# Spreading a routing chain over many steps, one pipeline for the output blocks, and loads a job ahead, in a one-core attention and routed-FFN kernel

## The chip, the cores and the metric

The kernel runs on one core of one Trainium2 chip, in one launch; the host only lays arrays out. The metric is the device time in microseconds of one execution, over several runs. A profiled execution has a span (first to last instruction) beside its own time.

## The reference

Two branches over the same tokens are mixed by a gate. S = 2048 tokens, D = 640, 32 heads of 20, four segments of 512 tokens. Cut to what matters:

```python
g = sigmoid((x * gate_w).sum(-1, keepdims=True))
# A: segment-wise attention with a compressive memory
q, k, v = x @ wq, x @ wk, x @ wv           # 32 heads of 20
for s in range(4):                         # segments of 512
    a_dot = softmax(qs @ ks.T * scale + causal_mask) @ vs
    a_mem = (phi(qs) @ M) / (phi(qs) @ z + 1e-6)
    o = sigmoid(beta) * a_mem + (1 - sigmoid(beta)) * a_dot
    M, z = M + phi(ks).T @ vs, z + phi(ks).sum()
a = o @ wo
# B: one routed token goes through a SwiGLU FFN (F = 1728)
r = x @ w_r
idx = argmax(r)
y = (silu(x[idx] @ w_gate) * (x[idx] @ w_up)) @ w_down * sigmoid(r[idx])
b = x + (y added at row idx)
return g * a + (1 - g) * b
```

All of it is float32; the large products are made from rounded high parts and remainders.

## The kernel before, in words

The work is cut into eight units u, each one half of the heads (16) in one segment of 512 tokens. A unit has nine projection jobs, T0 to T4 (rows of q and k, transposed, 512 tokens wide) and V0 to V3 (values, 128 tokens each), in the order `JOBS`. A job is 15 matmuls: five blocks of the 640 inputs, and for each the three products of high and low parts. High and low parts are made by `split`: ScalarE copies the loaded tile to the rounded type (hi), and VectorE or GpSimd subtracts it (lo). T weights come by `prepare_t`, V and O weights by `load_w` and `split_w`, x by `load_x` and `split_x`. In every one of these the load stands directly in front of the split. All loaded tiles (raw), and in the output stage the tiles ot and xf, share one ring of four buffers.

`evac_t` moves a finished T job out of PSUM: hi on ScalarE, lo on VectorE, then phi in three steps. `place` stores hi and lo to DRAM scratch (stkq, stkk) and `bring_back` loads them into the layout for attention (qs, ks). `keys`, `memory_read` and `memory_write` serve the compressive memory.

Attention runs over 32 groups n of four heads (four to a unit). A group has six slots: `a_step` makes scores for the row maxima, which VectorE reduces (mx); `m_rows` writes the negative maxima into qs by four small DMAs (qs<-mr); `b_step` makes the scores again, transposed and with the maxima subtracted, ScalarE takes the exponential, GpSimd masks the diagonal; `pv_phase` multiplies with the values in two halves (slots 1 and 5). `norm` divides, and `store` puts the result in the DRAM tensor otok.

TensorE's and SP's queues are in the order in which the Python program emits instructions; the other engines' order is set by the scheduler. The program interleaves generators by hand: `fill` lets the projections run ahead of the attention by a fixed lead, `extra` fills with output work, and `side` takes one step of the FFN in each half PV phase:

```python
def pv_phase(n, half):
    pv_step(n, half)
    for f in side:
        f.run(1.0)
```

At group 15 `route` finds the top token: a maximum per partition, a column out to DRAM (rrow<-best) and back as a row, a maximum, one value out and back to all partitions, twice over. At group 16 `fetch` loads that token's row and the FFN starts: `ffn_up` for gate and up (10 steps), `ffn_act`, `ffn_down` (8 steps, a pair of weight tiles wt each, from a ring of two buffers), then the row y goes to DRAM and comes back to all partitions (yb). At group 28 `finish()` emits what is left of it.

The output stage has 16 blocks t of 128 tokens. `row_load` loads otok's rows (ot), `out_load` loads x's rows (xf) and mixes them with the FFN's row, `out_rows` transposes and splits, `out_proj` runs 30 matmuls (L649) and stores. It treats four blocks at a time; inside the four, block t+1's loads are emitted at the start of block t, after the store of block t-1. Three fours run between the attention's instructions, the last four after its end.

## Time and profile before

| | |
|---|---|
| median of 3 runs | 819.74 us (819.0 to 822.08) |
| profiled execution, its own time | 825.51 us |
| its span | 823.8 us |
| TensorE busy | 691.1 us (84%) |
| VectorE, ScalarE, GpSimd busy | 442.0, 361.6, 188.7 us |
| mean granted TensorE clock | 0.901 of full |
| DMA | 116.30 MB, mean 141 GB/s |

In the views, PE is TensorE, PEld its weight load, DVE VectorE, ACT ScalarE, POOL GpSimd, SP the queue that issues all DMAs. L351 is line 351 of the kernel; `acc<-xhi,whi` names the tile written and the tiles read. A row of a timeline is: start in us, duration in us, engine, line, operation, tiles, shapes, count, and in brackets how long the engine was idle before and what released it. Rows of the chain that ended last have start, duration and what ran. A "releaser" is inferred from semaphores.

### The profile page before, as it was taken

Reading aid. Unit: us, or ns where it says so; the run is one execution under the profiler, and the core shown is the slowest. Engines: PE = TensorE matmul, PEld = TensorE weight load, DVE = VectorE, ACT = ScalarE, POOL = GpSimd, SP = SyncE. Lnnn points to the kernel's source line nnn. Section 1 sums busy time; section 2 is a strip of 40 time slices with the busy share of each in tenths; the row PEclk is TensorE's granted clock in tenths of the full one; section 3 lists DMA queues with packets and bytes.
Section 4 is the critical chain, followed back from the end, with each engine's and each line's share of the span. In section 5 each row is a group of like instructions: output and inputs, shape, how many; then the busy total and the mean of one; then the engine's idle time right before and its main releaser. Section 6 shows DMA issues by size and latency. Waiting matters only on the chain.

```text
span 823.8 us, 13347 instructions
## 1 busy us (share of the span) xinstructions
PE 691.1 (84%) x4496; PEld 468.9 (57%) x4496; DVE 442.0 (54%) x1523; ACT 361.6 (44%) x608; POOL 188.7 (23%) x297
## 2 busy tenths in 40 slices
PE   5478989989998997885598999898989588797876
PEld 3355566556665664553355665565656376475766
DVE  6426546655665775553355666674667355442323
ACT  4234545645564665541344455454545333242211
POOL 4002311522342233121131133323422111021000
PEclk9689989999998997897698999998999879797879
DMA  5546453644475474700786477547765612233323
GB/s 157 145 106 186 118 141 97 167 110 117 125 187 146 106 184 127 207 13 14 187 246 187 136 243 219 161 147 197 208 180 149 184 42 80 89 105 104 104 100 124
DMA packets 80627, 116.30 MB, mean 141 GB/s; under 512 B 37478, under 2 KB 41072, under 8 KB 80560
## 3 DMA queue, kind: packets, MB, share of 16 engines
q1 hardware_dynamic: 80560, 115.46, 49.7%
q8 instruction: 36, 0.59, 0.3%
q14 instruction: 31, 0.25, 0.1%
HBM read 72.94 MB, written 41.96 MB: 139 GB/s over the span
## 4 chain that ended last, share of the span: by engine, by line
PE 52%; DMA 19%; DVE 9%; ACT 7%; issue 6%; SPq 4%; POOL 1%; POOLq 0%; DVEq 0%; ACTq 0%
PE acc L351 13%; PE pv L454 7%; PE acc L649 7%; PE bt L434 7%; PE acc L356 7%; PE a L403 5%; DVE junk L406 3%; DMA xf<-in_x_dram 3%; DMA raw<-in_xT_dram 3%; DMA qs<-mr 3%; DMA stkq<-lo 3%; PE nm L266 3%; DVE lo L241 2%; DMA rrow<-best 2%; ACT hi L240 1%
## 5 line engine op out<-in xcount | busy, mean ns | idle before, releaser
L406 DVE CUSTOM_DVE_ANT_0 junk<-a,mask 128x512 bf16<-128x512 f32 (+3 forms) x512 | 250.2, 489 | 147.9 <-PE a L403 137.9
L438 ACT ACTIVATE p<-bt 128x768 f32<-128x768 f32 (+1 forms) x192 | 169.3, 882 | 187.0 <-PE bt L434 183.0
L441 POOL TENSOR_SCALAR_AFFINE_SELECT p<-p 128x256 f32<-128x256 f32 (+1 forms) x192 | 94.7, 493 | 402.3 <-ACT p L438 399.4
L434 PE MATMUL bt<-qs,ks 62*128 62x256 f32 (+2 forms) x512 | 100.0, 421 | 25.4 <-DMA qs<-mr 23.3
L351 PE MATMUL acc<-xhi,whi 128*128 128x512 f32 x200 | 89.7, 449 | 24.2 <-ACT xhi L149 15.1
L403 PE MATMUL a<-ks,qs 60*128 60x256 f32 (+2 forms) x512 | 84.7, 361 | 20.8 <-DVE mx L406 16.0
L351 PE MATMUL acc<-xhi,wlo 128*128 128x512 f32 x200 | 93.6, 468 | 0.5 <-DVE wlo L150 0.4
L434 PEld LDWEIGHTS bt<-qs,ks 62*128 62x128 f32 x512 | 47.1, 198 | 82.5 <-issue 41.5
L351 PE MATMUL acc<-xlo,whi 128*128 128x512 f32 x200 | 90.9, 454 | 1.6 <-POOL xlo L150 1.5
L454 PE MATMUL pv<-p,va 128*32 128x512 f32 (+3 forms) x1024 | 85.3, 452 | 0.0
L150 POOL TENSOR_TENSOR xlo<-raw,xhi 128x512 fp32r<-128x512 f32 x38 | 47.9, 1283 | 95.8 <-DMA raw<-in_xT_dram 62.4
L403 PEld LDWEIGHTS a<-ks,qs 60*128 60x128 f32 x512 | 50.3, 202 | 33.2 <-DVE mx L406 22.5
L351 PEld LDWEIGHTS acc<-xhi,whi 128*128 128x128 f32 x200 | 41.1, 206 | 45.9 <-ACT xhi L149 17.4
L649 PE MATMUL acc<-whi,oh 128*128 128x320 f32 x160 | 57.9, 362 | 4.9 <-ACT oh L626 3.4
L649 PE MATMUL acc<-whi,ol 128*128 128x320 f32 x160 | 56.1, 351 | 0.4 <-DVE ol L627 0.2
L356 PE MATMUL acc<-wlo,xhi 128*128 128x322 f32 (+1 forms) x160 | 56.2, 351 | 0.0
L351 PEld LDWEIGHTS acc<-xlo,whi 128*128 128x128 f32 x200 | 41.1, 205 | 25.2 <-issue 15.1
L356 PE MATMUL acc<-whi,xhi 128*128 128x322 f32 (+1 forms) x160 | 54.9, 343 | 0.0
L649 PE MATMUL acc<-wlo,oh 128*128 128x320 f32 x160 | 54.7, 342 | 0.0
L356 PE MATMUL acc<-whi,xlo 128*128 128x322 f32 (+1 forms) x160 | 52.4, 328 | 0.0
L351 PEld LDWEIGHTS acc<-xhi,wlo 128*128 128x128 f32 x200 | 41.5, 207 | 15.9 <-issue 10.1
L454 PEld LDWEIGHTS pv<-p,va 128*32 128x32 f32 x1024 | 27.4, 111 | 38.0 <-issue 29.0
(104 smaller groups left out, 932.7 us busy)
## 6 DMA issues: line engine op xcount, KB each, us to landing
qs<-stkq SPq DMA_DIRECT2D x64, 240.0 KB
ks<-stkk SPq DMA_DIRECT2D x64, 240.0 KB
raw<-in_xT_dram SPq DMA_DIRECT2D x40, 256.0 KB
stkq<-hi SPq DMA_DIRECT2D x32, 320.0 KB
stkq<-lo SPq DMA_DIRECT2D x32, 160.0 KB
otok<-ou SPq DMA_DIRECT2D x32, 160.0 KB
ot<-otok SPq DMA_DIRECT2D x16, 320.0 KB
xf<-in_x_dram SPq DMA_DIRECT2D x16, 320.0 KB
```

Source lines behind the costliest of these rows:

```text
L150: eng.tensor_tensor(out=lo, in0=raw, in1=f32(hi), op=OP.subtract)
L241: nc.vector.tensor_tensor(out=lo[:, :L], in0=acc, in1=f32(hi)[:, :L], op=OP.subtract)
L266: nc.tensor.matmul(nm[:, c, :], e[:GC, 128 * c:128 * c + 128], mbd[:, g, :], start=True, stop=True)
L351: nc.tensor.matmul(acc, a, b, start=i == 0, stop=i == 3 * KT - 1)
L356: nc.tensor.matmul(acc[:, :w], a, b, start=i == 0, stop=i == 3 * KT - 1)
L403: nc.tensor.matmul(a[:, b, at:at + nw], q_, k_, start=True, stop=True)
L406: nc.vector.tensor_tensor_reduce(out=junk[:, :w], in0=a[:, b, at:at + w], in1=mask[:, L - w:], scale=1.0, scalar=-3e38, op0=OP.add, op1=OP ...
L434: nc.tensor.matmul(bt[:, b, at:at + nw], k_, q_, start=True, stop=True)
L438: nc.scalar.activation(pt, bt[:, :, at:at + w], AF.Exp, scale=SCALE)
L441: nc.gpsimd.affine_select(out=d, in_=d, pattern=[[0, 2], [0, k], [1, 128]], base=0, channel_multiplier=-1, compare_op=OP.is_ge, fill=0.0)
L454: nc.tensor.matmul(pv[n][32 * j:32 * j + 32, L - w:], va[u % 2][:, c, VW * h:VW * h + 32], pt_tiles[n, j % 2, min(c, 2)][:, j // 2, at:at ...
L649: nc.tensor.matmul(acc[:, :n], a_[:, 128 * k:128 * k + 128], b_[:, n * b:n * b + n], start=i == 0, stop=i == 3 * KT - 1)
```

## The change

Five things are changed.

1. `prepare_t` is cut into `load_t` and `split_t`, and `prefetch` emits loads about one job ahead of their splits, for T, V, O weights and x. The first unit's subtractions stay on VectorE, the others move from VectorE to GpSimd.
2. In `evac_t` the last step of phi is put in a list `later` and emitted after the fourth matmul of the next job. `memory_read` takes its denominator straight from PSUM.
3. `route` becomes a generator with a step after each hop, and is the first part of `ffn`, which is now added to `side` at group 13. `ffn_act` and the end of `ffn_down` have steps between their DMAs.
4. `out_proj`, `out_first` and the call at the end become one generator `out_stage` over all 16 blocks. Loads go out up to two blocks ahead; the mixing of xf (`out_mix`) is emitted after six matmuls of its block, and a block's store after twelve matmuls of the next.
5. ot takes buffers of the x rings (in two pieces) in place of the raw ring.

The diff, cut to its core:

```diff
-    def prepare_t(hf, j, eng=None):
+    def load_t(hf, j):
 
         for kind, g in READY[j]:
             t = pool.tile([128, KT, 4, DH], F32, tag="raw", bufs=4, name="raw")
             nc.sync.dma_start(t.rearrange("p k j d -> p k (j d)"), columns(kind, hf, g, GC).rearrange("(k p) m -> p k m", p=128))
+            raws[kind, hf, g] = t
...
-                    split(h_.bitcast(F32R), l_.bitcast(F32R), src, eng or nc.vector)
+                    split(h_.bitcast(F32R), l_.bitcast(F32R), src, eng or nc.gpsimd)
...
-        split(hi[:, :raw.shape[1]], lo[:, :raw.shape[1]], raw, eng or nc.vector)
+        split(hi[:, :raw.shape[1]], lo[:, :raw.shape[1]], raw, eng or nc.gpsimd)
...
-            nc.vector.scalar_tensor_tensor(out=e, in0=acc, scalar=1.0, in1=e, op0=OP.add, op1=OP.max)
+            later.append(lambda: nc.vector.scalar_tensor_tensor(out=e, in0=acc, scalar=1.0, in1=e, op0=OP.add, op1=OP.max))
...
-        nc.vector.tensor_scalar(rm, t[:, :, :, DH], 1e-6, None, op0=OP.add)
+        nc.vector.tensor_scalar(rm, nm.rearrange("p c (j e) -> p c j e", e=VW)[:, :, :, DH], 1e-6, None, op0=OP.add)
...
-        if s == SEG - 1:
-            at = {"T1": 0, "T2": 1, "V0": 2, "V2": 3, "V3": 4}.get(job)
-            if at is not None and hf + 1 < NH:
-                prepare_t(hf + 1, at)
-            elif at is not None:
+        if u == 0:
+            if job == "T0":
+                load_t(0, 1)
+                split_t(0, 1, nc.vector)
+                load_t(0, 2)
+            elif job == "T1":
+                split_t(0, 2, nc.vector)
+            elif job == "T2":
+                split_v(0, (0, 1, 2, 3), nc.vector)
+                load_v(0, (4,))
+                load_t(0, 3)
+            elif job == "V0":
+                split_v(0, (4,), nc.vector)
+                split_t(0, 3)
+                load_t(0, 4)
+            elif job == "V1":
+                split_t(0, 4)
+        if u == SEG:
+            if job == "T0":
+                load_v(1, (0, 1, 2, 3))
+            elif job == "T1":
+                split_v(1, (0, 1, 2, 3))
+                load_v(1, (4,))
+            elif job == "T2":
+                split_v(1, (4,))
+        if s == SEG - 1 and hf + 1 < NH:
+            if job in ("T1", "T2", "V0", "V2", "V3"):
+                split_t(hf + 1, ("T1", "T2", "V0", "V2", "V3").index(job))
+            if job in ("T0", "T1", "T2", "V0", "V2"):
+                load_t(hf + 1, ("T0", "T1", "T2", "V0", "V2").index(job))
+        elif s == SEG - 1:
+            at = JOBS.index(job)
+            if at in (1, 2, 3, 4, 6):
+                split_w(("O", min(at, 5) - 1))
+            if at < KT:
                 load_w(("O", at))
-                split_w(("O", at))
         if u + 1 < NU:
-            for k in {"T4": (0, 1), "V3": (2, 3, 4)}.get(job, ()):
+            if job == "V2":
+                split_x(u + 1, 0)
+                split_x(u + 1, 1)
+            for k in {"T3": (0, 1), "T4": (2, 3), "V3": (4,)}.get(job, ()):
                 load_x(u + 1, k)
-                if k < 2:
-                    split_x(u + 1, k)
-        if u == 0:
-            j = {"T0": 1, "T1": 2, "V0": 3, "V1": 4}.get(job)
-            if j is not None:
-                prepare_t(0, j)
+
+    def load_v(hf, ks_):
+        for k in ks_:
+            load_w(("V", hf, k))
+
+    def split_v(hf, ks_, eng=None):
+        for k in ks_:
+            split_w(("V", hf, k), eng)
...
-                            if (u, job) in ((0, "T2"), (SEG, "T0")):
-                                for kk_ in range(KT):
-                                    load_w(("V", hf, kk_))
-                                    split_w(("V", hf, kk_))
+                            if (u, job) == (0, "T1"):
+                                load_v(0, (0, 1, 2, 3))
+                        if i == 4:
+                            while later:
+                                later.pop(0)()
...
-        ot[t] = pool.tile([128, D], F32, tag="raw", bufs=4, name="ot")
-        nc.sync.dma_start(ot[t], otok[128 * t:128 * t + 128, :])
+        ot[t] = (f32(pool.tile([128, L], F32R, tag="xhi", bufs=KT + 2, name="ot")),
+                 f32(pool.tile([128, L], F32R, tag="xlo", bufs=KT + 2, name="ot4"))[:, :128])
+        for o, c0, c1 in zip(ot[t], (0, L), (L, D)):
+            nc.sync.dma_start(o, otok[128 * t:128 * t + 128, c0:c1])
...
+        tops = []
+        for k in range(2):
+            if k == 0:
+                nc.vector.tensor_reduce(out=best[:, 0:1], in_=rg[:, 0, :], axis=AX.X, op=OP.max)
+            else:
+                nc.vector.scalar_tensor_tensor(out=cand, in0=rg[:, 0, :], scalar=tops[0], in1=tok, op0=OP.is_equal,
+                                               op1=OP.mult)
+                nc.vector.tensor_reduce(out=best[:, 1:2], in_=cand, axis=AX.X, op=OP.max)
+            yield 1
+            nc.sync.dma_start(rrow[k].rearrange("(p o) -> p o", o=1), best[:, k:k + 1])
+            yield 1
+            row = one.tile([1, 128], F32, name=f"row{k}")
+            nc.sync.dma_start(row, rrow[k:k + 1])
+            yield 1
+            top = one.tile([1, 1], F32, name=f"top{k}")
+            nc.vector.tensor_reduce(out=top, in_=row, axis=AX.X, op=OP.max)
+            if k == 1:
+                ix = one.tile([1, 1], I32, name="ix")
+                nc.vector.tensor_scalar(ix, top, -1.0, float(S), op0=OP.mult, op1=OP.add)
+                R["ix"] = ix
+            yield 1
+            nc.sync.dma_start(sel[:, k:k + 1], top)
+            yield 1
+            t = one.tile([128, 1], F32, name=f"all{k}")
+            nc.sync.dma_start(t, bass.AP(tensor=sel.tensor, offset=sel.offset + k, ap=[[0, 128], [1, 1]]))
+            tops.append(t)
...
+        yield 1
         nc.sync.dma_start(hrow.rearrange("o (j f) -> (o j) f", j=4), e.rearrange("(j r) f -> j r f", r=32)[:, 0, :])
+        yield 1
...
+        yield 1
         nc.sync.dma_start(yrow.rearrange("i (b f) -> (i b) f", b=2), y.rearrange("(b r) f -> b r f", r=32)[:, 0, :])
+        yield 1
...
+        yield 1
         nc.vector.tensor_tensor(out=yb, in0=yb, in1=y2, op=OP.add)
...
     def ffn():
+        yield from route()
+        fetch()
+        yield 1
         yield from ffn_up("fg", wg)
         yield from ffn_up("fu", wu)
-        ffn_act()
+        yield from ffn_act()
         yield 1
         yield from ffn_down()
...
+    def out_stage():
+        def can(t):
+            return t < S // 128 and ready[0] >= 4 * (SEG + t // 4) + 3
+
+        def loads(t):
+            if can(t) and t not in ot and t not in done_rows:
                 row_load(t)
                 out_load(t)
-                rows = out_rows(t)
+
+        n = D // 2
+        rows = {}
+        for t in range(S // 128):
+            while not can(t):
+                yield None
+            loads(t)
+            if t not in rows:
+                rows[t] = out_rows(t)
                 yield 400
-            hi, lo = rows
-            if t < 4 * s + 3:
-                row_load(t + 1)
-                out_load(t + 1)
+            loads(t + 1)
+            hi, lo = rows.pop(t)
             for b in range(2):
                 acc = psum.tile([128, 512], F32, tag="misc", bufs=3, name="acc")
-                n = D // 2
                 i = 0
                 for k in range(KT):
                     wh, wl = W["O", k]
                     for a_, b_ in ((hi, wh), (hi, wl), (lo, wh)):
-                        nc.tensor.matmul(acc[:, :n], a_[:, 128 * k:128 * k + 128], b_[:, n * b:n * b + n], start=i == 0, stop=i == 3 * KT - 1)
+                        nc.tensor.matmul(acc[:, :n], a_[:, 128 * k:128 * k + 128], b_[:, n * b:n * b + n], start=i == 0,
+                                         stop=i == 3 * KT - 1)
                         i += 1
                         yield n * COST_MM
-                    if b == 1 and k == 1 and t < 4 * s + 3:
-                        rows = out_rows(t + 1)
+                    if b == 0 and k == 1:
+                        out_mix(t)
+                    if b == 0 and k == 3 and t > 0:
+                        nc.sync.dma_start(out[128 * t - 128:128 * t, :], xf.pop(t - 1))
+                    if b == 1 and k == 1 and t + 1 in ot:
+                        rows[t + 1] = out_rows(t + 1)
+                        loads(t + 2)
                         yield 400
                 xs_ = xf[t][:, n * b:n * b + n]
                 nc.vector.scalar_tensor_tensor(out=xs_, in0=acc[:, :n], scalar=R["gx"][:, t:t + 1], in1=xs_,
                                                op0=OP.mult, op1=OP.add)
-            nc.sync.dma_start(out[128 * t:128 * t + 128, :], xf[t])
+        nc.sync.dma_start(out[S - 128:, :], xf.pop(S // 128 - 1))
...
-    prepare_t(0, 0)
+    load_t(0, 0)
+    load_x(0, 0)
+    load_x(0, 1)
+    split_t(0, 0, nc.vector)
     for k in range(KT):
-        load_x(0, k)
-        split_x(0, k, nc.vector if k % 2 else nc.gpsimd)
+        split_x(0, k, nc.gpsimd if k % 2 else nc.vector)
+        if k + 2 < KT:
+            load_x(0, k + 2)
...
-            if n == 15 and slot == 0:
-                route()
-            if n == 16 and slot == 0:
-                fetch()
+            if n == 13 and slot == 0:
                 side.append(Fill(ffn()))
             extra[:] = [f for f in extra if f.live]
             if n == 28 and slot == 0:
                 for f in side:
                     f.finish()
-                extra.append(Fill(out_first()))
+                extra.append(Fill(out_stage()))
...
-    Fill(out_proj(3)).finish()
```

## The prediction

> **What bounds the kernel now.** I read the page first, then a table of busy time by stage, then TensorE's own waits, then the stretches in which these waits lie. From the page: the engine shares, the granted clock in 40 slices, the chain that ended last.

> ```profile
> PE 691.1 (84%) x4496; PEld 468.9 (57%) x4496; DVE 442.0 (54%) x1523; ACT 361.6 (44%) x608; POOL 188.7 (23%) x297
> PEclk9689989999998997897698999998999879797879
> PE 52%; DMA 19%; DVE 9%; ACT 7%; issue 6%; SPq 4%; POOL 1%; POOLq 0%; DVEq 0%; ACTq 0%
> ```

> TensorE bounds the kernel: 691 of 823.8 us busy, no other engine above 54%. But 133 us are idle, and the clock falls where it idles. The table by stage (span, busy time of each engine, granted clock, DMA share) says where:

> ```profile
> 0.00:60.00 60.00, 34.58 (x117) 23.82 (x118) 26.40 (x60) 21.84 (x41) 9.05 (x16) 0.83 0.53 136
> 60.00:356.00 296.00, 269.87 (x1783) 175.27 (x1782) 179.86 (x684) 157.84 (x266) 86.33 (x132) 0.94 0.53 142
> 356.00:402.00 46.00, 22.79 (x143) 14.20 (x142) 13.90 (x59) 10.71 (x19) 6.26 (x11) 0.74 0.23 58
> 402.00:640.00 238.00, 222.52 (x1588) 142.44 (x1590) 148.42 (x527) 118.90 (x196) 69.96 (x109) 0.95 0.65 187
> 640.00:660.00 20.00, 9.38 (x64) 5.74 (x58) 7.99 (x22) 7.65 (x13) 1.48 (x3) 0.78 0.62 180
> 660.00:758.00 98.00, 82.28 (x510) 63.77 (x511) 44.95 (x136) 33.60 (x54) 13.90 (x26) 0.85 0.27 88
> 758.00:823.80 65.80, 49.66 (x303) 43.69 (x302) 20.48 (x39) 11.08 (x22) 1.68 (x3) 0.86 0.30 103
> ```

> Idle: 25 us at the start, 23 around the routing, 11 at 640 to 660, 32 in the output stage (660 on), 42 spread over the 534 us of the two middle stretches. TensorE's longest waits (total, times, longest) name the causes, and all of them but the third are transfers or what follows one:

> ```profile
> PE ttp L624 <- DMA ot<-otok: 29.6, 8, 10.1
> PE bt L434 <- DMA qs<-mr: 23.3, 4, 19.1
> PE a L403 <- DVE mx L406: 16.0, 19, 4.1
> PE acc L351 <- ACT xhi L149: 15.1, 8, 7.2
> ```

> I cost the change by these stages. The profiled execution took 825.51 us (span 823.8 and 1.7 around it), 5.8 above the median of 819.74. I make the sum on 825.51 and carry the difference over to the median.

> **Routing chain.** Two TensorE waits of the timeline, and two pieces of the chain that ended last:

> ```profile
> 369.66 0.79 PE L403 MATMUL a<-ks,qs 60*128 60x256 f32 x4 [4.07 <-DVE mx L406]
> 401.26 1.17 PE L434 MATMUL bt<-qs,ks 62*128 62x512 f32 x2 [19.14 <-DMA qs<-mr]
> 358.12 8.29 DMA rrow<-best
> 376.82 7.14 DMA rrow<-best
> ```

> All of route() is emitted at group 15, so SP waits in line for each hop (column out 8.29 and 7.14 us) with the next jobs' stores and the maxima (qs<-mr) queued behind it. The change puts one hop into each half PV phase, two per group. A group takes about 18 us (the 534 us of middle stretches for 29 groups), so the phases are some 6 and 12 us apart: a hop of 8 us holds SP for 2 us at worst, the one of 2 to 3 us not at all. The 4.07 + 19.14 = 23.2 us of waits go; I leave 1 for the remnants: **-22** (-16 with two held hops and a late mr, -27 if the clock of 0.74 also rises).

> **FFN tail.** The FFN steps run one per half PV phase. Counted in the code: 12 for routing, 1 fetch, 10 for gate and up, 3 around the activation, 8 pairs of down weights, 3 for the row y: 37. From group 13 to 28 there are 30 phases; before it was 19 steps in 24. At group 28 finish() emits what is left in one piece: the fourth pair's matmuls and then four whole rounds of load, matmul, load. The weight ring has two buffers, so a pair's load waits for the matmuls of the pair before, and TensorE, in order, stands. The rows for a round: SP's issue of one pair, its landing in the chain, its eight matmuls, and what follows (y out, yb in); last, the wait that stands at this place now.

> ```profile
> 592.98 0.72 SPq L545 DMA_DIRECT2D wt<-in_wd_dram  x2
> 592.98 4.09 DMA wt<-in_wd_dram
> 585.00 0.54 PE ffn L588 x8
> 610.45 0.53 SPq L591 DMA_DIRECT2D yrow<-y  x1
> 612.26 0.34 SPq L595 DMA_DIRECT2D yb<-yrow  x1
> 657.11 1.33 PE L624 MATMUL ttp<-identf,ot 128*128 128x128 f32 x5 [10.12 <-DMA ot<-otok]
> wt<-in_wd_dram SPq DMA_DIRECT2D x16, 270.0 KB
> ```

> A round is 4.09 from the first issue, 0.36 for the second of the pair, 0.54 of matmuls: 5.0; four are 20. Then y goes out and back (612.26 - 610.45 = 1.8) before SP reaches the first ot load, so the 10.12 us wait behind it stays about as it is; I take 2 off, as the other engines have caught up by then: **+18**. Bounds: +4 if the rounds swallow the whole ttp wait and a pair lands in 3, +28 if landings take 5.5 and the ttp wait grows by the y hop. [...]

> **Output stage.** SP's wait for the finished rows, three TensorE waits, and a run of output matmuls at full clock:

> ```profile
> SPq L658 <- DVE xf L656: 88.1, 13, 14.9
> 693.94 0.66 PE L473 MATMUL otp<-identf,pvs 128*128 128x128 f32 x4 [1.60 <-DVE ol L627]
> 750.79 1.30 PE L624 MATMUL ttp<-identf,ot 128*128 128x128 f32 x5 [4.34 <-DMA ot<-otok]
> 791.93 1.30 PE L624 MATMUL ttp<-identf,ot 128*128 128x128 f32 x5 [4.21 <-DMA ot<-otok]
> 813.88 5.97 PE acc L649 x39
> ```

> Each block's store stands in SP's queue in front of the next block's loads, and every fourth block loads with nothing ahead. In the change loads go out two blocks ahead, the store of a block follows twelve matmuls into the next, the mixing on ScalarE no longer heads its queue while xf travels, and the boundaries every four blocks vanish (the last four still need the last group; some 50 matmuls lie between, 50 x 0.153 = 7.7 us). One load becomes two, 16 issues of 0.4 us on a queue that waits 88 us here anyway. What remains is TensorE's work: busy time times clock, 82.28 x 0.85 + 49.66 x 0.86 = 113, and 823.8 - 819.85 = 4 after the last matmul: 117 of 163.8. Of the 47 between I keep 13 for waits that no load causes (the 1.60 is one) and for the clock after them: **-34** (-17 if only the boundary waits go, -44 if hardly any idle is left).

> **Start.** TensorE's waits and SP's block of V loads:

> ```profile
> 22.76 0.50 PE L351 MATMUL acc<-xhi,whi 128*128 128x512 f32 x1 [3.31 <-ACT whi L149]
> 29.92 0.72 PE L403 MATMUL a<-ks,qs 60*128 60x512 f32 x1 [2.88 <-DMA ks<-stkk]
> 53.74 0.65 PE L351 MATMUL acc<-xhi,whi 128*128 128x512 f32 x1 [4.90 <-ACT whi L149]
> 26.43 8.56 SPq L144 DMA_DIRECT2D raw<-in_wc_dram  x15
> 83.05 0.50 PE L351 MATMUL acc<-xhi,whi 128*128 128x512 f32 x1 [2.45 <-ACT xhi L149]
> ```

> T2's and T3's weights come a job earlier, so the 3.31 and 4.90 go. But in the order in which the built kernel queues its DMAs, twelve V issues now stand ahead of T1's stores and five more ahead of ks0's return, 17 x 0.57 = 9.7 us, of which the earlier start hides some 4: the first a step comes about 5 later. Five V subtractions between its maxima move out of the way (-2). 5 - 2 - 4.9 and the clock: **-3** (-9 if SP is through by then, +6 if it is not and T3 waits again). The 2.45 at 83.05 belongs to the next part.

> **Middle.** The x loads go out a job ahead. Of the 15.1 us behind xhi, 7.2 are the kernel's first load; the other 7.9 go, and I let SP's eight V loads ahead of one mr and late subtractions eat 1: **-7**. The moved subtractions: 25 more instructions stand on POOL in the built order.

> ```profile
> L150 POOL TENSOR_TENSOR xlo<-raw,xhi x3: 1278/1285/1387, 7.2 to 12.5; 128x512 fp32r<-128x512 f32 x3
> L150 DVE TENSOR_TENSOR xlo<-raw,xhi x2: 677/703/729, 9.3 to 11.3; 128x512 fp32r<-128x512 f32 x2
> 38.95 0.69 DVE L406 CUSTOM_DVE_ANT_0 junk<-a,mask 128x512 bf16<-128x512 f32 x1 [0.18 <-PE a L403]
> 71.42 2.52 POOL L150 TENSOR_TENSOR xlo<-raw,xhi 128x512 fp32r<-128x512 f32 x2 [57.59 <-DMA raw<-in_xT_dram]
> 72.90 0.69 DVE L406 CUSTOM_DVE_ANT_0 junk<-a,mask 128x512 bf16<-128x512 f32 x1 [0.96 <-PE a L403]
> ```

> They take 1285 ns in place of 703, 25 x 1.3 = 32 us on an engine busy 189 of 824, in jobs ahead of their use: nothing on the path. The deferred phi frees VectorE of a wait for ScalarE and takes no work away; the rm from PSUM likewise: 0, between -6 and +3.

> **Sum:** -22 + 18 - 34 - 3 - 7 = -48: 825.5 becomes 777.5, and on the median 819.7 becomes **772**.

> **Rivals.** *Output bound elsewhere:* the block is held by its chain of transpose, ScalarE copy, VectorE subtraction and only the boundary waits go: -17 in place of -34, 789. For it: waits behind ol and oh already exist; against: they are 1 to 2 us. *FFN rounds hidden:* SP and TensorE are out of step and the rounds take the place of the ttp wait, +4: 758. Against it: the matmul queue is in order, nothing stands between. [...] *Slower:* early loads wait on SP for one of four raw buffers and the maxima (qs<-mr) stand behind them; bt then waits in each of the 32 groups. At 1.5 us each the whole gain of 48 is gone, at 2 it is 16 us slower: 836. For it: bt already waits for qs<-mr where SP is late. Against: in the built order most groups have the same loads ahead of their mr as now, and only one has eight.

> **Numbers.** Forecast 0.55 (its own range 757 to 788), output bound elsewhere 0.18, POOL 0.06, FFN hidden 0.13 (together 0.92, all faster), slower 0.06 and 0.02 for nothing that shows. The range 748 to 800 takes in the first four with their bounds and leaves out the slower case and the far ends. A measurement of this kernel tells 0.5% from no change, about 4 us: faster 0.92, same 0.02, slower 0.06.

> **What would show it.** Right: no 19 us wait of bt near 400; at group 28 four waits of ffn for wt of 4 us each; ttp's wait for ot near 0 after the first; the clock in the output stage above 0.95. Wrong: bt's wait for qs<-mr grown over many groups, DVE subtractions or maxima longer than now, output blocks still above 6 us each.

## The result, and the profile after

The changed kernel takes 761.32 us (median of 4 runs, 758.56 to 763.38) against 820.91 us (median of 4, 819.0 to 829.87) for the kernel before: a ratio of 0.9252, 95% interval 0.9177 to 0.9327. The forecast was 772, range 748 to 800. The profiled execution took 758.56 us, its span is 756.6. So the spans differ by 67.2 us and the medians by 59.6: the profiled run of before lay 4.6 above its median, that of after 2.8 below. Medians and spreads here and below are over all runs; the ratios leave out the few that took over 1.5% more than the fastest of the same kernel.

The page of the changed kernel, engine shares and granted clock in 40 slices:

```profile
PE 662.8 (88%) x4496; PEld 448.6 (59%) x4496; DVE 428.1 (57%) x1498; ACT 356.8 (47%) x608; POOL 213.9 (28%) x322
PEclk9669999999999899999968999999999755999999
```

TensorE is at 88% of a shorter span, and the last quarter shows nines except for one hole (7, 5, 5). To see where the time went, both spans are cut at the same work, not at the same time: at the start of the transposition of the maxima (mtp) of groups 0, 13, 15, 17, 28 and 29. Columns as in the table by stage. Before:

```profile
0.00:66.05 66.05, 39.18 (x137) 27.01 (x138) 30.92 (x79) 23.50 (x44) 9.05 (x16) 0.83 0.55 142
66.05:309.55 243.50, 225.90 (x1534) 148.16 (x1532) 149.20 (x574) 131.71 (x220) 73.44 (x114) 0.95 0.53 139
309.55:353.93 44.38, 37.33 (x218) 22.55 (x217) 24.64 (x88) 23.00 (x41) 11.70 (x17) 0.85 0.55 153
353.93:412.08 58.15, 34.91 (x217) 22.67 (x215) 22.06 (x87) 18.51 (x32) 10.41 (x17) 0.77 0.29 76
412.08:635.45 223.37, 207.89 (x1492) 132.05 (x1490) 138.91 (x493) 110.64 (x183) 64.48 (x100) 0.95 0.65 188
635.45:672.33 36.88, 24.65 (x146) 18.43 (x144) 17.66 (x58) 13.21 (x22) 6.34 (x11) 0.77 0.44 122
672.33:823.80 151.47, 121.22 (x762) 98.07 (x762) 58.60 (x150) 41.05 (x69) 13.25 (x24) 0.87 0.31 102
```

After:

```profile
0.00:66.67 66.67, 36.79 (x137) 26.27 (x138) 30.65 (x73) 23.88 (x46) 14.10 (x21) 0.78 0.56 146
66.67:298.27 231.60, 217.96 (x1533) 144.70 (x1532) 144.23 (x565) 129.94 (x221) 83.96 (x126) 0.98 0.56 148
298.27:334.48 36.21, 31.97 (x217) 19.91 (x216) 22.36 (x82) 20.86 (x38) 12.85 (x20) 1.00 0.65 154
334.48:366.27 31.79, 30.83 (x218) 19.72 (x215) 20.94 (x86) 18.91 (x35) 13.26 (x20) 1.00 0.60 164
366.27:584.48 218.21, 202.34 (x1443) 129.64 (x1442) 131.64 (x483) 109.89 (x183) 69.46 (x102) 0.95 0.64 175
584.48:645.00 60.52, 38.67 (x194) 21.64 (x192) 21.52 (x65) 12.88 (x22) 6.36 (x11) 0.66 0.49 143
645.00:756.60 111.60, 104.28 (x762) 86.67 (x762) 56.72 (x149) 40.45 (x68) 13.95 (x24) 1.00 0.43 132
```

The counts of PE instructions agree row by row, but for the two rows between which 48 FFN matmuls have moved. Beside the forecast:

| stretch (to group) | before | after | difference | forecast |
|---|---|---|---|---|
| start (to 0) | 66.05 | 66.67 | +0.6 | -3 |
| 0 to 13, 13 to 15, 17 to 28 | 511.25 | 486.02 | -25.2 | -7 (middle) |
| 15 to 17, routing | 58.15 | 31.79 | -26.4 | -22 |
| 28 to 29, FFN tail | 36.88 | 60.52 | +23.6 | +18 |
| 29 to the end, output | 151.47 | 111.60 | -39.9 | -34 |
| sum | 823.8 | 756.6 | -67.2 | -48 |

The timeline at group 28: TensorE's waits for the FFN's last four pairs of weights and before the first block's transposes, and SP's loads of these pairs (x4 is half a pair; the second halves of the third and fourth pair have rows of their own, of which the last is shown):

```profile
601.57 2.10 PE L640 MATMUL ffn<-wt,ht 108*32 108x320 f32 x8 [5.53 <-DMA wt<-in_wd_dram]
606.03 2.68 PE L640 MATMUL ffn<-wt,ht 108*32 108x320 f32 x8 [2.36 <-DMA wt<-in_wd_dram]
610.39 1.28 PE L640 MATMUL ffn<-wt,ht 108*32 108x320 f32 x4 [1.68 <-DMA wt<-in_wd_dram]
614.75 1.28 PE L640 MATMUL ffn<-wt,ht 108*32 108x320 f32 x4 [1.19 <-DMA wt<-in_wd_dram]
616.58 1.28 PE L640 MATMUL ffn<-wt,ht 108*32 108x320 f32 x4 [0.55 <-DMA wt<-in_wd_dram]
629.81 1.30 PE L685 MATMUL ttp<-identf,ot 128*128 128x128 f32 x5 [8.37 <-DMA ot<-otok]
596.92 16.98 SPq L595 DMA_DIRECT2D wt<-in_wd_dram  x8
```

Rounds of load and matmul, 4.4 us from one to the next (606.03 - 601.57, 610.39 - 606.03, 614.75 - 610.39), as forecast in kind, in front of a ttp wait that has lost 1.8 of its 10.12.

The start of the changed kernel, SP's queue, and the wait that it leads to:

```profile
19.95 5.61 SPq L144 DMA_DIRECT2D raw<-in_wc_dram  x12
28.96 1.32 SPq L144 DMA_DIRECT2D raw<-in_wc_dram  x3
32.40 0.85 SPq L239 DMA_DIRECT2D ks<-stkk  x2
37.75 0.79 PE L446 MATMUL a<-ks,qs 60*128 60x512 f32 x1 [13.37 <-DMA ks<-stkk]
```

The first keys are asked for at 32.40 (25.59 before) and the first scores start at 37.75 (29.92 before).

### The profile page after: what moved, and what is told of

Same layout as the page of the kernel before. It is cut to its first block, busy times and chain, and to the rows that moved or that the text cites. A ratio compares the mean times of both kernels' runs of the same rounds, so it can differ in the third digit from the quotient of the medians.

```text
span 756.6 us, 13400 instructions
## 1 busy us (share of the span) xinstructions
PE 662.8 (88%) x4496; PEld 448.6 (59%) x4496; DVE 428.1 (57%) x1498; ACT 356.8 (47%) x608; POOL 213.9 (28%) x322
## 4 chain that ended last, share of the span: by engine, by line
PE 67%; DMA 13%; DVE 6%; ACT 6%; issue 5%; SPq 3%; POOL 0%; POOLq 0%; ACTq 0%
PE acc L391 17%; PE acc L396 9%; PE pv L497 9%; PE bt L477 9%; PE acc L721 7%; PE a L446 6%; PE nm L272 3%; DVE junk L449 2%; DMA wt<-in_wd_dram 2%; DMA wt<-in_wu_dram 2%; DVE lo L247 2%; DMA raw<-in_wc_dram 2%; PE ktp L263 2%; PE otp L518 1%; ACT hi L246 1%
## 5 line engine op out<-in xcount | busy, mean ns | idle before, releaser
L446 PE MATMUL a<-ks,qs 60*128 60x256 f32 (+2 forms) x512 | 81.5, 349 | 26.3 <-DMA ks<-stkk 13.5
L477 PE MATMUL bt<-qs,ks 62*128 62x256 f32 (+2 forms) x512 | 95.8, 407 | 7.2 <-ACT p L481 5.0
L391 PE MATMUL acc<-xhi,whi 128*128 128x512 f32 x200 | 86.8, 434 | 10.0 <-ACT xhi L149 7.7
L391 PE MATMUL acc<-xhi,wlo 128*128 128x512 f32 x200 | 91.1, 456 | 0.0
L391 PE MATMUL acc<-xlo,whi 128*128 128x512 f32 x200 | 87.5, 438 | 0.0
L477 PEld LDWEIGHTS bt<-qs,ks 62*128 62x128 f32 x512 | 44.5, 189 | 62.1 <-issue 40.7
L446 PEld LDWEIGHTS a<-ks,qs 60*128 60x128 f32 x512 | 48.6, 193 | 37.3 <-DMA ks<-stkk 13.8
L721 PE MATMUL acc<-whi,oh 128*128 128x320 f32 x160 | 53.2, 332 | 1.7 <-DVE ol L689 1.5
L150 POOL TENSOR_TENSOR xlo<-raw,xhi 128x512 fp32r<-128x512 f32 x37 | 47.3, 1290 | 19.3 <-ACT xhi L149 18.1
L391 PEld LDWEIGHTS acc<-xlo,whi 128*128 128x128 f32 x200 | 39.8, 199 | 20.8 <-issue 14.7
L721 PE MATMUL acc<-whi,ol 128*128 128x320 f32 x160 | 51.5, 322 | 0.0
L721 PE MATMUL acc<-wlo,oh 128*128 128x320 f32 x160 | 50.3, 314 | 0.0
L391 PEld LDWEIGHTS acc<-xhi,wlo 128*128 128x128 f32 x200 | 40.3, 202 | 13.6 <-issue 9.7
```

The lines of the kernel that those rows point to most:

```text
L150: eng.tensor_tensor(out=lo, in0=raw, in1=f32(hi), op=OP.subtract)
L391: nc.tensor.matmul(acc, a, b, start=i == 0, stop=i == 3 * KT - 1)
L446: nc.tensor.matmul(a[:, b, at:at + nw], q_, k_, start=True, stop=True)
L477: nc.tensor.matmul(bt[:, b, at:at + nw], k_, q_, start=True, stop=True)
L721: nc.tensor.matmul(acc[:, :n], a_[:, 128 * k:128 * k + 128], b_[:, n * b:n * b + n], start=i == 0, stop=i == 3 * KT - 1)
```

## The experiments

All times of before beside these runs lie at 810.76 to 826.73, medians 816.3 to 820.8. "The changed kernel" means its 761.32 and the table above. It was not run again beside the experiments, and the medians of before differ by 4.6 us from one series to another (816.3 to 820.9), so these runs don't tell a difference under some 5 us between two kernels.

**One part alone: the output stage.** The kernel before with `row_load` and the functions from `out_load` to `out_stage` of the change.

```diff
-    def out_proj(s): ...
+    def out_stage(): ...
-    Fill(out_proj(3)).finish()
```

> The kernel before with the new output stage alone (one pipeline, early loads, late stores, ot in the x rings). Theory (the output stage's waits are transfers): from group 29's transposition of the maxima to the end 112 to 118 us in place of 151.5, the whole 780 to 788. Rival (blocks are held by their chain of transpose, copy and subtraction; the changed kernel's gain there comes from elsewhere): 130 to 140 us, the whole 800 to 808.

Measured: 779.49 us (776.66 to 781.09), ratio 0.9498 (0.9427 to 0.9568). Group 29 to the end:

```profile
667.11:778.90 111.79, 104.39 (x762) 86.62 (x762) 56.91 (x149) 40.48 (x68) 13.95 (x24) 1.00 0.42 132
```

111.8 us in place of 151.5, the same as in the changed kernel (111.6): this part carries its 40 us by itself, idle 30.2 to 7.4, and the same matmuls busy for 104.4 in place of 121.2 at a clock of 1.00 in place of 0.87. Both marks came out a little under what I had expected (112 and 780). The rival with blocks held by their own chain falls.

**One part alone: the routing steps and the FFN's.**

```diff
-            if n == 15 and slot == 0:
-                route()
-            if n == 16 and slot == 0:
-                fetch()
+            if n == 13 and slot == 0:
                 side.append(Fill(ffn()))
```

(with the change's `route`, `ffn_act`, `ffn_down` and `ffn`)

> The kernel before with the third part of the change alone: the routing chain as steps, the FFN's other steps, start at group 13. Theory (the parts add): 26 us less between groups 15 and 17, 15 to 24 more between 28 and 29, the whole 806 to 819. Rival (the tail's price hangs on the new output stage): the stretch from 28 to 29 as before (36.9), the whole 790 to 797. Other rival (the routing gain needs the loads ahead too): under 15 us less between 15 and 17, the whole above 822.

Measured: 811.62 us (806.84 to 818.55), ratio 0.9879 (0.9801 to 0.9957). Groups 15 to 17, and 28 to 29:

```profile
354.85:385.49 30.64, 30.62 (x218) 19.77 (x215) 20.98 (x85) 18.42 (x32) 10.40 (x17) 1.00 0.56 149
604.06:667.96 63.90, 38.41 (x194) 21.75 (x192) 22.04 (x66) 13.71 (x23) 6.34 (x11) 0.65 0.45 135
```

27.5 less in the first, 27.0 more in the second (I had expected 15 to 24): this part puts in at one place what it takes out of another. The prediction's two terms are real and, by these marks, nearly cancel. With the output stage's 38.6 and this kernel's 6.5 in medians, some 15 of the whole 59.6 are left for the loads ahead and the engines of the splits.

**Loads at their splits.** The changed kernel with the order of loads of before.

```diff
-            if job == "V2":
-                split_x(u + 1, 0)
-                split_x(u + 1, 1)
-            for k in {"T3": (0, 1), "T4": (2, 3), "V3": (4,)}.get(job, ()):
+            for k in {"T4": (0, 1), "V3": (2, 3, 4)}.get(job, ()):
                 load_x(u + 1, k)
+                if k < 2:
+                    split_x(u + 1, k)
```

(likewise for T, V and O weights; four subtractions of the first unit's T3 and T4 weights, which the changed kernel has on GpSimd, are on VectorE here)

> The changed kernel with every load of T, V, O weights and x emitted directly in front of its split, as in the kernel before; engines of the splits as in the change. Theory (the 18 us that the change gained beside output stage and routing come from the loads ahead): group 14's transposition of the maxima at 328 to 336 in place of 316, the whole 773 to 781. Rival (they come from VectorE's freed queue: subtractions on GpSimd, late phi): 759 to 766. Forecast of the prediction: 10 us, 771.

Measured: 776.01 us (772.44 to 782.22), 14.7 slower than the changed kernel; the ratio to the kernel before is 0.9472 (0.9385 to 0.9559) in place of 0.9252 (0.9177 to 0.9327). Groups 13 to 15:

```profile
308.64:352.21 43.57, 37.37 (x217) 22.82 (x216) 21.59 (x82) 22.99 (x41) 16.55 (x23) 0.84 0.60 149
```

43.6 and a clock of 0.84, as before (44.4, 0.85), against 36.2 and 1.00 in the changed kernel. The loads ahead are worth about 15 us in the changed kernel, and the rival, which left them nothing, falls. Of the 7.4 lost in this stretch only 2.0 are idle time (43.57 - 37.37 against 36.21 - 31.97); 5.4 are the same matmuls taking longer.

**Splits back on VectorE.**

```diff
-                    split(h_.bitcast(F32R), l_.bitcast(F32R), src, eng or nc.gpsimd)
+                    split(h_.bitcast(F32R), l_.bitcast(F32R), src, eng or nc.vector)
...
-        split(hi[:, :raw.shape[1]], lo[:, :raw.shape[1]], raw, eng or nc.gpsimd)
+        split(hi[:, :raw.shape[1]], lo[:, :raw.shape[1]], raw, eng or nc.vector)
```

> The changed kernel with the weights' subtractions of the later units back on VectorE (25 instructions). The prediction put the move at nothing: 758 to 764. [...] Other rival (the move is what freed VectorE's queue): group 14 later by 4 us or more, the whole 766 to 775.

Measured: 770.25 us (769.36 to 775.24), 8.9 slower; the two sets of runs do not overlap, and the ratio to the kernel before is 0.9419 (0.9347 to 0.9491). Groups 13 to 15, where the second half's V and T weights are split:

```profile
302.73:342.75 40.02, 33.77 (x217) 20.78 (x216) 24.20 (x87) 21.10 (x38) 8.68 (x15) 0.96 0.60 146
```

3.8 of the loss lie here: the changed kernel and the next three experiments, which leave loads and splits of these groups as they are in it, all take 36.2 there. In groups 0 to 13 this kernel's 234.8 lies inside the 231.6 to 238.3 of kernels with the splits on GpSimd, which tells nothing. The move to GpSimd is a gain, which I had at nothing; where the rest of it lies is not shown. I took it for the waits of the scores for the maxima, in the waits of TensorE (total, times, longest) with these splits on VectorE,

```profile
PE a L446 <- DVE mx L449: 11.3, 13, 2.2
```

and in the changed kernel:

```profile
PE a L446 <- DVE mx L449: 8.1, 10, 1.8
```

Three microseconds less waiting, for a gain of 9; but TensorE's waits of mtp for ou (L523) are 3.9 longer in the changed kernel (13.1 in place of 9.2). So the waits do not show by which way the gain comes. This gain and that of the loads ahead can't be added: 14.7 and 8.9 make 24, and 15 are left for the two. No run undoes both.

**Phi at once.**

```diff
-            later.append(lambda: nc.vector.scalar_tensor_tensor(out=e, in0=acc, scalar=1.0, in1=e, op0=OP.add, op1=OP.max))
+            nc.vector.scalar_tensor_tensor(out=e, in0=acc, scalar=1.0, in1=e, op0=OP.add, op1=OP.max)
```

> The changed kernel with the last step of phi emitted at once in evac_t, as in the kernel before. The prediction put the move at nothing: 758 to 764, and the groups 2 and 3 of each unit (20.0 and 19.5 us where undisturbed) as they are. Rival (VectorE waits for ScalarE's two steps with the maxima behind it): these groups 1 to 2 us longer in units 0 to 2 and 4 to 6, 8 to 15 us in all, 768 to 776.

Measured: 761.19 us (756.49 to 762.48). No difference: within the 5 us that these runs tell, this edit is worth nothing, as forecast.

**V loads behind the first keys.**

```diff
-                            if (u, job) == (0, "T1"):
+                            if (u, job) == (0, "T2"):
                                 load_v(0, (0, 1, 2, 3))
```

(with the splits moved from T2 to V0)

> The changed kernel with the first unit's V loads emitted behind the return of ks0 (after the sixth matmul of T2, as in the kernel before) and their splits a job later. Theory (SP's queue: the V issues hold the first keys up): TensorE's wait of 13.4 us for ks<-stkk falls to 3 to 6 us, group 0's transposition of the maxima comes at 58 to 62 in place of 66.7, the whole is 753 to 757. Rival (the first job after the scores waits for the V weights or T3's instead): group 0 earlier, group 1 (81.2) unchanged, the whole 760 to 763.

Measured: 760.94 us (759.29 to 769.16), no difference that these runs tell. TensorE's waits:

```profile
31.77 0.79 PE L447 MATMUL a<-ks,qs 60*128 60x512 f32 x1 [8.19 <-DMA ks<-stkk]
51.84 0.63 PE L397 MATMUL acc<-whi,xhi 128*128 128x322 f32 x1 [5.68 <-ACT whi L149]
```

The scores start 6 us earlier, and V0 then waits 5.7 for its weights; group 0 comes at 67.2 in place of 66.7 and group 1 at 85.4 in place of 81.2. SP's queue is what delays the keys, but the V weights that stand in front of them are needed as urgently. The rival has the cause and the time right, though it had put group 0 earlier and group 1 unchanged; the 13 us wait is no 13 us of gain.

**Taking the tail away, first try.** One more FFN step per group from group 20 on.

```diff
+            if n >= 20 and slot == 3:
+                for f in side:
+                    f.run(1.0)
```

> The changed kernel with one more FFN step per group (slot 3) from group 20 on: 8 more steps, so the 37 steps are through before group 28 and finish() emits nothing. Theory (the tail is a row of load-matmul rounds in TensorE's order): the stretch from group 28's transposition of the maxima to group 29's, 60.5 us in the changed kernel, falls to 36 to 42, and the whole to 738 to 745. Rival (the rounds only fill the time in which the first ttp waits for ot anyway): the stretch stays above 50, the whole at 752 to 758. Second rival (three steps a group are too close for a weight pair to land): ffn waits for wt of 2 us or more in each group from 20 on, and the gain is under 10 us.

Measured: 764.96 us (759.46 to 768.1), no gain. Groups 22 to 28, and 28 to 29:

```profile
472.93:619.18 146.25, 127.87 (x835) 76.42 (x835) 77.83 (x268) 59.94 (x99) 43.11 (x60) 0.89 0.59 168
619.18:654.67 35.49, 25.17 (x146) 18.62 (x144) 18.11 (x59) 12.49 (x21) 6.62 (x11) 0.76 0.53 148
```

Groups 22 to 28 in the changed kernel:

```profile
468.20:584.48 116.28, 107.74 (x794) 69.05 (x795) 73.32 (x263) 59.94 (x99) 43.05 (x60) 0.99 0.66 190
```

The tail is gone (35.5), and all of it is back in the groups ahead of it (146.3 in place of 116.3). The idle time grew by 9.8 (18.4 against 8.5), the busy time by 20.1 for 41 more matmul records, at a clock of 0.89 in place of 0.99. The second rival is right that the gain is lost, but three of ffn's waits for wt there are 2 us or more (2.1, 2.8, 2.0), not one in each group: most of the loss is busy time, at the lower clock.

**Second try: groups 13 to 19.**

```diff
+            if 13 <= n < 20 and slot == 3:
+                for f in side:
+                    f.run(1.0)
```

> The changed kernel with one more FFN step per group (slot 3) from group 13 to 19, in place of from 20 on: 7 more steps, mostly of the routing chain, so that the 37 are through when group 28 comes, and the weight pairs have the changed kernel's distance from group 20 on. Theory (three weight steps a group are too close, as groups 22 to 28 of the first experiment show with 120 us in place of 95; hops are not): the stretch from group 28 to 29 is 35 to 38 us, the groups 13 to 19 lose 0 to 8 together, the whole is 738 to 748. Rival (a step on the path costs about 3 us wherever it stands, so that the 24 us come back in the earlier groups): 755 to 765.

Measured: 759.68 us (752.42 to 765.57), no gain that these runs tell. TensorE's waits, and groups 18 to 21:

```profile
403.70 2.70 PE L612 MATMUL ffn<-wt,xs 128*32 128x432 f32 x8 [4.39 <-DMA wt<-in_wg_dram]
430.11 2.69 PE L612 MATMUL ffn<-wt,xs 128*32 128x432 f32 x8 [3.52 <-DMA wt<-in_wg_dram]
456.73 2.75 PE L612 MATMUL ffn<-wt,xs 128*32 128x432 f32 x8 [5.13 <-DMA wt<-in_wu_dram]
```

```profile
392.46:470.55 78.09, 63.98 (x422) 36.98 (x423) 36.65 (x132) 29.41 (x51) 15.68 (x25) 0.89 0.63 186
```

These groups took 59.1 in the changed kernel (446.75 - 387.64). The tail is 32.3, 28 less. My theory held for the tail and for group 21 on, and failed in assuming that only routing hops lie in groups 13 to 19: the gate's weight pairs begin there, three to a group, and each of the groups 18 to 20 pays with a wait of 3.5 to 5.1 us. (The 120 and 95 us that I expected from are groups 23 to 28 of the first try and of the changed kernel.)

**Third and fourth: pack only the hops.** In `route` each maximum and its store to DRAM become one step (four steps less):

```diff
                 nc.vector.tensor_reduce(out=best[:, 1:2], in_=cand, axis=AX.X, op=OP.max)
-            yield 1
             nc.sync.dma_start(rrow[k].rearrange("(p o) -> p o", o=1), best[:, k:k + 1])
...
                 R["ix"] = ix
-            yield 1
             nc.sync.dma_start(sel[:, k:k + 1], top)
```

> The changed kernel with four steps less in the routing chain (each maximum and its store to DRAM in one step), everything else in the changed kernel's places: 33 steps, so that group 28 finds only the last pair's matmuls and the y row left, no round. Theory (hops can be packed, weight pairs can't): the stretch from group 28 to 29 is 36 to 42 us in place of 60, groups 13 to 18 lose 0 to 4, groups 19 to 28 nothing, the whole 738 to 745. Rival (whatever is taken from the tail comes back earlier, as in the two kernels with more steps): 755 to 762.

Or one more step, halfway between the two others, only where the hops are:

```diff
             if n >= 0 and slot == 5:
                 pv_phase(n, 0)
+            if 13 <= n < 17 and slot == 3:
+                for f in side:
+                    f.run(1.0)
```

> The changed kernel with one more step per group only in groups 13 to 16, which hold the twelve routing hops, and ahead of that slot's fill, halfway between the two others. Theory: as with merged hops, 28 to 29 at 36 to 42; SP is held by a column store of 7 to 8 us in steps about 5 us apart, 2 to 6 us lost in groups 15 to 17; the whole 740 to 748. Rival: 755 to 762.

Measured: 750.54 us (748.03 to 751.03) and 743.15 us (742.42 to 751.89), ratios 0.9137 (0.9073 to 0.9201) and 0.9092 (0.901 to 0.9175). With even hops, groups 15 to 17 and 28 to 29:

```profile
340.89:377.29 36.40, 32.78 (x217) 20.62 (x215) 21.45 (x88) 19.25 (x35) 13.06 (x20) 0.95 0.56 138
591.15:628.64 37.49, 24.17 (x161) 16.36 (x160) 19.27 (x61) 12.79 (x22) 6.92 (x11) 0.82 0.56 171
```

The tail falls by 23.0, the hops take back 4.6 (36.4 in place of 31.8), inside the 2 to 6 expected. Merged hops take back more, 8.7 in the same groups (381.61 - 341.12 = 40.5), mostly one wait:

```profile
370.61 1.16 PE L477 MATMUL bt<-qs,ks 62*128 62x512 f32 x2 [7.42 <-DMA qs<-mr]
```

That is the wait that the change removed (19.14 then), come back in small, where I had expected 0 to 4 in all; the whole, too, lies above the 738 to 745 expected for it. SP's queue in front of it:

```profile
351.82 0.32 SPq L552 DMA_DIRECT2D rrow<-best  x1
...
354.99 0.42 SPq L226 DMA_DIRECT2D stkk<-lo  x1
362.71 0.77 SPq L239 DMA_DIRECT2D qs<-stkq  x2
```

SP issues nothing for 7.3 us between the stores behind a column store and the return of the stored rows, and the maxima (qs<-mr) follow that return. That the column store (8.29 and 7.14 us in the kernel before) is what holds those stores up is read from the times, not shown by a run. Together the four kernels say what the tail is worth: nothing where the weight steps pay for it, 11 (merged) to 18 us (even) where the hops do.

**The first output block's loads ahead of its transposes.**

```diff
             loads(t)
+            if t == 0:
+                loads(1)
+                for _ in range(8):
+                    yield None
             if t not in rows:
```

> Merged hops, and in the output stage the first two blocks' loads emitted eight fills ahead of the first transposes. Theory: TensorE's wait for ot at the first ttp (8.4 us in the changed kernel) falls under 2 us; the filling work then lies later; 6 to 12 us off merged hops alone, 728 to 738. Rival (the gap is filled elsewhere, since groups 28 and 29 have too little other work without the blocks): within 3 us of merged hops.

> Even hops and the lag together. Theory (the two act in different places, groups 15 to 17 and the first output block): 11 us off even hops, as the lag took off merged hops, 729 to 735, under 0.90 of the kernel before. Rival (they share the gap behind group 28): 740 to 743.

Measured: 739.85 us (734.79 to 741.73) with merged hops, 10.7 less than without and a little above the 738 expected at most, and with even hops 731.57 us (median of 6, 725.6 to 735.65), ratio 0.8968 (0.8918 to 0.9017) to the kernel before. Even hops with the lag, the first ttp, and group 28 to the end:

```profile
615.57 0.77 PE L685 MATMUL ttp<-identf,ot 128*128 128x128 f32 x5 [0.69 <-DMA ot<-otok]
```

```profile
589.78:729.20 139.42, 129.50 (x923) 103.36 (x921) 75.96 (x209) 53.72 (x90) 20.21 (x35) 0.98 0.50 152
```

The wait of 8.4 (11.4 with even hops alone) is 0.7, and the stretch takes 139.4 in place of 149.4 (740.5 - 591.15). This version beats both kernels; it is 30 us faster than the changed one.

## Why the prediction was right, and where its terms were off

The measured time lies 11 us under the forecast and inside the range and inside the forecast's own 757 to 788. The mechanisms of the three large terms are as forecast. That the sum comes so near is in part luck: in the profiles, routing, middle and output gained 28.5 more than their terms, start and tail lost 9.2 more. Of its steps:

- **Routing, -22.** Measured -26.4, and -27.5 by itself, at the -27 end of the bounds, which I had tied to the clock: it went from 0.77 to 1.00. Idle time fell from 23.2 to 1.0, as priced; the other 4.1 are busy time for the same matmuls (34.91 to 30.83) at that higher clock. The steps cost nothing while two a group; bt's waits for qs<-mr are 2.0 us in all after. The step sizes that I worried about (a hop of 8 us) show only when hops are packed.
- **FFN tail, +18.** Measured +23.6, +27.0 by itself; bounds +4 to +28. The four rounds take 21.0 us from the first load's issue (596.92) to the end of the last matmuls (616.58 + 1.28), where I put 20, but two terms are off and nearly cancel: the matmuls of a pair take 2.1 to 2.7 us and not 0.54, and the waits that I announced at 4 us each are 5.5, 2.4, 1.7 and 1.2, or 11.9 in all with those between the halves of a pair. What I left out is the clock, 0.50 from 598 to 617.8: the stretch has 9.6 us more idle (21.85 against 12.23) but also 14.0 more busy time. By an estimate 3 of these are the six pairs that moved there, at the 0.54 of before; the other 11 came with the clock at 0.50, and how much of them is due to it is not shown.
- **Output stage, -34.** Measured -39.9. Its floor was TensorE's work at full clock, and I kept 13 us for waits and clock; 7.3 us of idle are left (111.60 - 104.28) and the clock is at 1.00.
- **Start, -3.** Measured +0.6. The mechanism was there, the size off: 17 issues ahead of ks0's return, first scores 7.8 later and not 5. T2's and T3's waits are gone, which pays for it.
- **Middle, -7.** Measured -25.2: this is the term that was mis-sized, and by the profiles it makes up the distance to the forecast (18.2 of 19.2; the other errors nearly cancel). I added up waits at their own length (7.9 behind xhi). Idle time in the three stretches (span less busy time) fell from 17.6 + 7.1 + 15.5 = 40.1 to 13.6 + 4.2 + 15.9 = 33.8, by 6.4, near the forecast. The other 18.9 are busy time: about 3 of it FFN matmuls that moved behind group 28 (six pairs of 0.54), and some 16 for the most part the same matmuls run faster, at clocks of 0.98 and 1.00 where it was 0.95 and 0.85. In groups 0 to 13 some of this is luck of one execution: seven kernels have the same instructions up to group 13, and their profiles take 231.6 to 238.3 us there, the changed kernel's being the shortest. The longest, the first try's, has the clock of before:

```profile
65.97:304.22 238.25, 224.10 (x1533) 148.43 (x1532) 143.98 (x564) 129.96 (x221) 83.93 (x126) 0.95 0.55 144
```

  The kernel before and the two with one part alone take 242.0 to 246.2, so there is a gain, but up to 7 of the -25.2 are chance; the medians moved by 8 us less than the two profiles. That loads directly in front of their splits bring the clock back down to 0.84 in groups 13 to 15 is shown by the experiment; the small waits' shares in the rest are not.
- **Moved subtractions, 0 (-6 to +3).** By the experiment about -9, outside my bounds; part of it stands in the middle's -25.2. I asked what they cost on GpSimd (nothing) and not what they had cost on VectorE. That they stood there in front of maxima on which TensorE waits is argued; the waits do not show it.
- **Deferred phi, 0.** Right by the experiment, within its 5 us.

Of the rivals, the output stage did not stay bound elsewhere, the FFN rounds were not hidden, and SP was not blocked by early loads. The 0.06 for POOL stood for GpSimd's subtractions holding VectorE up: no run shows them doing so, and with the weights' subtractions back on VectorE the kernel takes 8.9 us more. In the kernel before a maximum took 0.69 us beside a subtraction on GpSimd (at 72.90) and 0.69 with GpSimd idle (at 38.95). The groups of the maxima on the page of before and of after, mean ns of one in the last number ahead of the idle time:

```profile
L406 DVE CUSTOM_DVE_ANT_0 junk<-a,mask 128x512 bf16<-128x512 f32 (+3 forms) x512 | 250.2, 489 | 147.9 <-PE a L403 137.9
```

```profile
L449 DVE CUSTOM_DVE_ANT_0 junk<-a,mask 128x512 bf16<-128x512 f32 (+3 forms) x512 | 249.9, 488 | 132.8 <-PE a L446 123.0
```

489 and 488 ns, with GpSimd's busy time up from 188.7 to 213.9: the maxima were not held up. VectorE's other instructions are not compared.

## What to carry to other kernels

Price a short TensorE wait at more than its length where the clock falls behind it (to 0.50 behind one of 1.39 us in one profile, not in another), and cut two traces at the same work, not at the same time, before comparing them; in the two profiles the middle stretches gained three times what their listed waits added up to, part of it by chance, and groups 13 to 15, where four profiles agree on 36.2 us (41.4 and 44.4 with the middle of before), gained 5 to 8 us for 2 to 3 of idle time. Before a gain of a few microseconds is read from one profile, a second one of the same instructions belongs beside it. When a long dependent chain is spread over steps, count the steps against the places that are left: what does not fit comes back as a serial tail, and it can only be packed where a step is light (hops, which took back 4.6 or 8.7 us here) and not where each step must wait for a transfer (weight pairs, with waits of 3.5 to 5.1 us). A wait that a view names can be moved without gain: the 13 us at the start and the tail's 24 us both came back elsewhere when they were merely shifted.

## What the runs showed of the hardware

Behind the same wait of 1.39 us, a group took 19.5 us in one profile and 22.5 in another. Group 6's transposition of the maxima has the same idle time in two kernels whose instructions up to there are the same. The changed kernel (that row, and busy times and clock of the 3.4 us around it):

```profile
171.87 0.22 PE L462 MATMUL mtp<-identr,mneg 128*66 128x128 f32 x1 [1.39 <-DVE ou L523]
170.83:174.25 3.42, 2.04 (x14) 1.41 (x14) 1.54 (x4) 1.35 (x4) 0.97 (x2) 1.00 0.55 154
```

The kernel with more FFN steps from group 20 on, which differs only later (that row, the 3.4 us around it and the next):

```profile
174.29 0.22 PE L462 MATMUL mtp<-identr,mneg 128*66 128x128 f32 x1 [1.39 <-DVE ou L523]
173.06:176.47 3.41, 1.84 (x12) 1.32 (x14) 1.73 (x5) 1.54 (x4) 1.16 (x2) 1.00 0.60 169
176.47:179.88 3.41, 3.41 (x17) 2.88 (x14) 1.47 (x6) 1.25 (x2) 0.64 (x1) 0.50 0.35 101
```

After 1.39 us of idle time the clock stayed at 1.00 in the one and fell to 0.50 in the other, from 176.47 to 183.30; the group took 19.5 us in the one and 22.5 in the other. In the 3.41 us around the wait TensorE was busy for 2.04 us in the one and for 1.84 in the other.

For readers of profiles: the same group of the same instructions differed by 3.0 us between two executions, with the clock at 1.00 in one and at 0.50 for 6.8 us in the other, and a difference of that size in one group of one profile tells nothing.
